# Transposes moved between VectorE and TensorE, and FFN pieces dealt by a table, in an RWKV-7 and hard-swish kernel

## The chip, the cores and the metric

The kernel runs on one core of a Trainium2 chip. The core has a matrix engine (TensorE, called PE in the profile; PEld is its weight load), a vector engine (VectorE, DVE), a scalar engine (ScalarE, ACT), GpSimd (POOL) and SyncE (SP), which only issues transfers. TensorE writes its results to PSUM; the other engines read them from there. Each engine runs its own instructions in the order of the program and waits for others by semaphores. The metric is the device time of one execution in microseconds (us).

## The reference

Six inputs r, k, v, w, a, b of shape (batch 4, heads 8, time 768, width 40) go through a recurrence over time. Its output is the input of a feed-forward layer (FFN) with hard-swish. All is float32.

```python
for t in range(S):
    kt, vt, rt = (k[:, :, t], v[:, :, t], r[:, :, t])
    wt, at, bt = (w[:, :, t], a[:, :, t], b[:, :, t])
    y[:, :, t] = np.einsum('bhd,bhde->bhe', rt, state)
    Sa = np.einsum('bhde,bhe->bhd', state, at)
    state_decay = state * wt[:, :, None, :] - np.einsum('bhd,bhe->bhde', Sa, bt)
    state = state_decay + np.einsum('bhd,bhe->bhde', vt, kt)
...
h = x @ w_in                                   # (3072, 320) @ (320, 2048)
g = h * np.clip(h + 3.0, 0.0, 6.0) / 6.0
return (g @ w_out).astype(np.float32)          # (3072, 2048) @ (2048, 320)
```

## The kernel before

Time is cut into 12 chunks of 64 steps and the batch into two pairs: 24 units, numbered 0 to 23, each one chunk of one pair with all 8 heads. `NU` = 4 units (two chunks of both pairs) form a group; `NK` = 24.

**A unit's work** has two halves, each a set of named stages. A stage is a generator: it issues TensorE's matmuls, yields, and then issues what empties PSUM.

`prepare(i)` needs no state and runs ahead. W turns w (time by width to width by time) and starts a cumulative product along time (a scan on VectorE); `gam` finishes the products `G` and their reciprocals `rg`. A, B and K turn a, b, k and multiply by these. F is the matrix a·b of a chunk, E is a·k with a mask, EV is E times v, `factor` makes the scaled k and b for the update of the state.

`step(i)` is the part with the state. RT and VT turn r and v; RT also scales the state. S turns the state; R is a times the state plus EV; U and UT apply the inverse of (1 + F) to R; C and H are masked products of r with v and with U; rS is r times the state; y adds up the output and the new state; `move` and `move2` carry the output into the FFN's layout `xt` by eight transfers, four from ScalarE's queue and four from SyncE's. `beside` copies v.

**Turns.** There are three ways to turn a matrix. `turn_pairs` (L524) is four whole 128x128 TensorE transposes into one PSUM bank. `turn_halves` (L534) is eight of half the rows, into a pair of banks shared through `ps_pair`. `turn_blocks` (L475, L478) is VectorE's own transpose in blocks of 32x32; it needs its input loaded in another layout by `fetch_blocks` (L464), which reads everything twice, with eight transfers for r and four for a instead of four and two. `blocked(name, i)` says from which unit on this way is used.

**The inverse** of a group of four units is made on VectorE by `invert`: a transpose `fb`, then 60 small products and sums (L801, L807), two transposes. It is a generator too and is advanced by `aside(n)`, n steps at a time. Two `third_block` parts follow on TensorE in the first two units of the next group.

**The FFN** is the generator `stream`. A job is half of the hidden width of one unit: `expand` (matmuls `h`, L1144; ScalarE's `gt`, L1159; VectorE's `gt`, L1160) and `contract` (matmuls `o`, L1185). It yields after some matmuls; what lies between two yields is called a piece. Eight pieces make a job. A unit's jobs can begin when its `move2` is issued. `pieces(n)` keeps a fraction and deals whole pieces.

**Order.** The first units are written out by hand. From unit 4 on, a loop goes over `i` and four blocks `j` per unit; m counts the blocks, 0 to 79. In a block, `a_block(m)` collects the stages due for the unit's own step (`OWN_STAGES`, six stages over six blocks, so that two units overlap) and for the units prepared ahead (`AHEAD_STAGES` or `CLOSE_STAGES`), in two parts: those that began at a block divisible by four, and the others. `together` first issues all matmuls of a part in the order `PRODUCTS`, then everything else in the order `RESULTS`. At most five PSUM banks are handed out before it empties what it has. Stages named in `TURNS` get a PSUM bank from a ring (`one` or half a pair); the others share pairs of banks. After the first part come half of the block's FFN pieces, then the second part, the third block if there is one, and the other half. The number of pieces follows from `rate`: 2.8, 3.5 or 4.5 a block, 6.2 while an inversion is under way, then with two or three inversion steps after each piece; the fraction is carried, and once `spread` is set (from unit 7) it counts 8/9.

Unit u from 8 on is prepared from block max(3(u - 8), 4(u - 9)) on.

Of the kernel before, what the change touches and what calls it, by code (L numbers as in the profile page):

```python
# [11 lines left out]
ALU = mybir.AluOpType  # L12
# [19 lines left out]
def kernel(  # L32
# [402 lines left out]

    def blocked(name, i):

        return i >= {"A": 2 * NU, "R": NU + 1}.get(name, NK)

    def fetch_blocks(name, x, b, g, fresh):  # L440

# [38 lines left out]
    def fetch(name, i, engine=None):  # L480

        if i is None or i >= NK:
            return
        x, crossed = {"W": (w, 0), "A": (a, 0), "B": (b, 0), "K": (k, 0), "R": (r, 1),
                      "V": (v, 1)}[name]
        if name == "V":
            t = values[i % AHEAD]
        else:
            t = placed.get((name, i))
            if (name, i) == ("R", 1):  # L490
                t = others["K"]
            t = t if t is not None else (others if i < 2 * NU and i % 2 and name != "R" else inputs)[name]
        g, p = names[i]
        if blocked(name, i):
            t = fetch_blocks(name, x, 2 * p, g, i == (NU + 1 if crossed else 2 * NU))
            data[i][name + "N"] = t
            return
        engines = engine or nc.sync
        for q in range(2):
            engine = engines[q] if isinstance(engines, tuple) else engines  # L500
            y = x[2 * p + q, :, g * BL:(g + 1) * BL, :]
            rows = slice(q * BL, (q + 1) * BL)
            if crossed:
                for s in range(2):
                    engine.dma_start(out=t[rows, 4 * s:4 * s + 4, 0:D],
                                     in_=y[s::2].rearrange("h t e -> t h e"))
            else:
                engine.dma_start(out=t[rows, :, 0:D], in_=y.rearrange("h t e -> t h e"))
        data[i][name + "N"] = t
# [69 lines left out]
    def prepare(i, F):  # L579
# [56 lines left out]

        def a_stage():
            at = o["at"] = grp.tile([P, NPR, P], F32, name="at", tag="at")
            if halves:
                nc.vector.memset(_ap(o["wm"][:], 0, [[HB + 1, 2 * NB + 1]]), 0.0)  # L640
                turn_blocks(at, o["AN"], "A")
                nc.gpsimd.tensor_tensor(out=at[:], in0=at[:], in1=o["G"][:], op=ALU.mult)  # L642
            else:
                x = turn_pairs(o["AN"])
                yield PE
                nc.vector.memset(_ap(o["wm"][:], 0, [[HB + 1, 2 * NB + 1]]), 0.0)
                nc.vector.tensor_tensor(out=at[:], in0=x[:], in1=o["G"][:], op=ALU.mult)
            fetch("A", following(i))

        def b_stage():  # L650
# [78 lines left out]
                fetch(name, following(i))  # L729

        def k_stage():
            x = turn_in(o["KN"], halves)
            yield PE
            kt = o["kt"] = turned("kt")
            for y, z, g in zip(parts_of(kt, halves), x, parts_of(o["rg"], halves)):
                nc.vector.tensor_tensor(out=y, in0=z, in1=g, op=ALU.mult)  # L736

        def e_stage():
# [141 lines left out]
    def step(i):  # L880
# [50 lines left out]

        def s_S():

            sp = ps_pair(4, SLOT) if halves else ps_any([P, 2, 2, P])
            for q in range(2):
                for j in range(2):
                    x = st[:, q, 2 * j:2 * j + 2, :].rearrange("p r d -> p (r d)")
                    if halves:
                        for s in range(2):
                            nc.tensor.transpose(out=sp[s][:, 2 * q + j, :], in_=x[half(s)],  # L940
                                                identity=ident[half(s), half(s)])
                    else:
                        nc.tensor.transpose(out=sp[:, q, j, :], in_=x, identity=ident[:])
            yield PE
            S = m["S"] = grp.tile([P, 2, 2, P], F32, name="S", tag="S", bufs=1)
            if halves:
                nc.scalar.activation(out=S[:].rearrange("p q j (s e) -> p s (q j) e", s=2), in_=sp[2], func=AF.Copy)  # L947
            else:
                nc.scalar.activation(out=S[:], in_=sp[:], func=AF.Copy)
# [141 lines left out]
        def s_move2():  # L1091
            for dst, src in m["moves"][4:]:
# [1 line left out]
            ready[i] = m["xt"]  # L1094
            yield from ()

        return {"RT": s_RT, "RT0": s_RT, "R": s_R, "VT": s_VT, "S": s_S, "U": s_U, "C": s_C, "UT": s_UT,
                "rS": s_rS,
                "sn": s_sn, "H": s_H, "y": s_y_sn if halves else s_y, "beside": s_beside, "move": s_move, "move2": s_move2}

# [294 lines left out]
    for _ in range(18):  # L1395
# [4 lines left out]

    OWN_STAGES = [["RT", "VT"], ["R", "C", "S", "beside"], ["U", "UT", "rS"], ["H"], ["y"],
                  ["move", "move2"]]
# [11 lines left out]
    FIRST_NARROW = PRODUCTS[len(TURNS)]  # L1416

    def together(stages):

        begun, banks = [], 0  # L1420

        def finish():
# [9 lines left out]
        for name in PRODUCTS:  # L1432
            if name == FIRST_NARROW and narrow and spread[0] and stages:
                narrow[0]()
            for stage in stages.get(name, []):
                if name in TURNS:
                    need = 2 * (open_half[0] is None) if ring[0][0] == "pair" else 1
                else:
                    width = WIDTH.get(name, NPR * BL)
                    need = 2 * (shared[0] is None or shared[1] + width > 512)  # L1440
                if banks + need > 5:
                    finish()
                    banks, need = 0, 1 if name in TURNS else 2
                banks += need
                rest = stage()
                next(rest)
                begun.append((name, rest))
        begun.extend((name, stage()) for name in stages if name not in PRODUCTS
                     for stage in stages[name])
        finish()  # L1450

# [3 lines left out]
    def a_block(m):  # L1455
# [4 lines left out]
            ahead[u, m] = prepared(u), CLOSE_STAGES if close else AHEAD_STAGES  # L1460
        if m % BLOCKS == 0 and m // BLOCKS + NU < NK:
            i = m // BLOCKS + NU
            first = [["RT" if blocked("R", i) else "RT0", "VT"]]
            own[i, m] = step(i), first + OWN_STAGES[1:]
# [24 lines left out]
    m = 0  # L1489
    for i in range(NU, NK):  # L1490
        spread[0] = i >= 2 * NU - 1
        for j in range(BLOCKS):
            rate, inversion = 3.5, 0
            if i + AHEAD >= NK + NU - 1:
                rate = 4.5
            if i < 2 * NU - 1:
                rate = 2.8
            parts = a_block(m)
            next(parts)
            if side or i % NU == NU - 1 and rate < 4:  # L1500
# [12 lines left out]
            m += 1  # L1513
    for _ in range(2):
        for _ in a_block(m):
# [35 lines left out]
```

## Time and profile before

| what | value |
|---|---|
| median of 3 runs | 803.71 us (803.26 to 806.04) |
| the profiled execution | 804.22 us, span 802.5 us |
| TensorE busy | 721.0 us, 90% of the span |
| VectorE busy | 510.0 us, 64% |
| ScalarE, GpSimd busy | 298.5 us (37%), 171.8 us (21%) |
| FFN matmuls `h` and `o` | 252.1 and 233.7 us of TensorE |
| inversion steps (L801, L807) | 66.5 and 66.5 us of VectorE |
| r's and a's VectorE transposes (L475, L478) | 14.3 and 11.1 us |
| mean granted TensorE clock | 0.953 |

The profile gives for each engine when it was busy, for each group of instructions its line, operation, operands, count, busy time and the mean of one, and for idle time the instruction that ended it. Busy time of a group of overlapping matmuls is the time that at least one of them ran, so it is less than count times mean. The granted clock is the share of full speed that TensorE was allowed.

### The profile page before, as it was taken

To read this page: it belongs to the slowest core of one execution; us is meant where nothing else is said; L and a number is where in the kernel's file an instruction comes from. 1 tells how busy PE (TensorE), PEld (TensorE's weight loads), DVE (VectorE), ACT (ScalarE), POOL (GpSimd) and SP (SyncE) were. 2 spreads that over 40 slices of the span, in tenths; PEclk is the share of its full clock that TensorE was granted. 3 is DMA by queue.
4 is the path that set the end of the run, shared out by engine and by line. 5 is a ranking of instruction groups with operands and counts; after the bars stand their busy time and mean duration, and the time that the engine had idled before them with its cause. 6 is when DMAs were issued, how large, how long until landed. Compare 5 with 4: busy or idle time off the path is not lost.

```text
span 802.5 us, 32704 instructions
## 1 busy us (share of the span) xinstructions
PE 721.0 (90%) x14416; PEld 604.6 (75%) x14416; DVE 510.0 (64%) x1024; ACT 298.5 (37%) x629; POOL 171.8 (21%) x316
## 2 busy tenths in 40 slices
PE   5735778999979989999999999999999999999998
PEld 4625666878757878787878778878778888888876
DVE  7898886688545599564799455899345983333110
ACT  2337661232533414443334442324443224322121
POOL 6403012321233321222212112213112202000000
PEclk9756978999989999999999999999999999999999
DMA  8673653420434331443323334323333112210000
GB/s 121 133 181 93 153 137 64 70 48 15 80 67 75 74 65 35 84 81 68 64 62 54 61 79 79 62 58 62 58 78 71 20 29 45 46 38 18 20 19 16
DMA packets 196733, 53.87 MB, mean 67 GB/s; under 512 B 179952, under 2 KB 195312, under 8 KB 196592
## 3 DMA queue, kind: packets, MB, share of 16 engines
q1 hardware_dynamic: 188968, 48.43, 31.0%
q10 hardware_dynamic: 7624, 3.36, 1.6%
q8 instruction: 113, 1.85, 1.0%
q14 instruction: 28, 0.23, 0.1%
HBM read 39.81 MB, written 3.93 MB: 55 GB/s over the span
## 4 chain that ended last, share of the span: by engine, by line
PE 55%; DVE 21%; issue 9%; DMA 5%; SPq 4%; ACT 3%; POOL 2%; ACTq 1%; POOLq 0%; DVEq 0%
PE h L1144 20%; PE o L1185 17%; PE pair L562 3%; DVE prod L801 3%; DVE x L807 3%; SPq L464 3%; PE pair L1040 3%; DVE prods L599 2%; DVE gt L1160 2%; DVE wm L610 2%; PE pair L958 1%; DMA W<-in_w_dram 1%; PE pair L534 1%; ACTq L1088 1%; PE pair L978 1%
## 5 line engine op out<-in xcount | busy, mean ns | idle before, releaser
L1144 PE MATMUL h<-xt,win 128*128 128x128 f32 (+1 forms) x2304 | 252.1, 284 | 8.0 <-DVE gt L1160 7.9
L1144 PEld LDWEIGHTS h<-xt,win 128*128 128x128 f32 (+1 forms) x2304 | 232.6, 193 | 26.5 <-issue 6.7
L1185 PE MATMUL o<-wout,gt 128*128 128x320 f32 x768 | 233.7, 448 | 0.0
L1185 PEld LDWEIGHTS o<-wout,gt 128*128 128x128 f32 x768 | 140.3, 193 | 52.0 <-issue 2.4
L1160 DVE SCALAR_TENSOR_TENSOR gt<-gt,h 128x512 f32<-128x512 f32 x96 | 62.1, 682 | 66.3 <-ACT gt L1159 66.0
L1159 ACT ACTIVATE gt<-h,three 128x512 f32<-128x512 f32 x96 | 62.4, 685 | 106.6 <-PE h L1144 82.0
L801 DVE TENSOR_TENSOR prod<-x 128x30 f32<-128x30 f32 (+9 forms) x180 | 66.5, 369 | 8.9 <-POOL x L786 3.4
L807 DVE TENSOR_TENSOR x<-x,prod 128x30 f32<-128x30 f32 (+9 forms) x180 | 66.5, 370 | 5.5
L1048 POOL TENSOR_TENSOR yg<-ys,gam 128x512 f32<-128x512 f32 x20 | 25.4, 1271 | 135.7 <-DVE ys L1047 95.6
L575 DVE COPY_PREDICATED store<-mask,pair 128x512 f32<-128x512 int32 x40 | 29.1, 727 | 31.8 <-PE pair L562 21.7
L722 POOL TENSOR_TENSOR KBt<-K,rgt 128x320 f32<-128x320 f32 x19 | 16.9, 887 | 146.8 <-ACT rgt L711 141.0
L599 DVE TENSOR_TENSOR_SCAN prods<-wm,start 128x528 f32<-128x528 f32 x24 | 33.6, 1406 | 17.7 <-ACT wm L596 17.3
L736 DVE TENSOR_TENSOR kt<-pair,rgam 128x512 f32<-128x512 f32 x19 | 13.1, 687 | 48.8 <-PE pair L702 48.4
L642 POOL TENSOR_TENSOR at<-at,gam 128x512 f32<-128x512 f32 x16 | 20.4, 1272 | 81.3 <-DVE at L478 77.4
L1047 DVE TENSOR_TENSOR ys<-pair,ys 128x512 f32<-128x512 f32 x20 | 13.8, 689 | 36.5 <-PE pair L1040 36.5
L755 ACT ACTIVATE EV<-pair 64x320 f32<-64x320 f32 x44 | 18.9, 431 | 40.1 <-PE pair L750 32.2
L1040 PE MATMUL pair<-store,KBt 64*64 64x104 f32 x1280 | 32.6, 250 | 0.5 <-DVE bt L655 0.5
L610 DVE TENSOR_TENSOR_SCAN wm<-wm,start 128x528 f32<-128x528 f32 x24 | 30.4, 1268 | 0.8
L1040 PEld LDWEIGHTS pair<-store,KBt 64*64 64x64 f32 x1280 | 29.2, 133 | 1.1 <-DVE bt L655 0.6
L1203 ACT ACTIVATE ob<-o 128x320 f32<-128x320 f32 x22 | 9.6, 436 | 53.9 <-PE o L1185 29.9
L869 ACT ACTIVATE tinv<-pair 32x256 f32<-32x256 f32 x48 | 18.0, 374 | 25.6 <-DMA xt<-yg 17.7
L947 ACT ACTIVATE S<-pair 128x512 f32<-128x512 f32 x20 | 11.9, 597 | 37.9 <-PE pair L534 22.2
(284 smaller groups left out, 1036.7 us busy)
## 6 DMA issues: line engine op xcount, KB each, us to landing
R<-in_r_dram SPq DMA_DIRECT2D x168, 40.0 KB
A<-in_a_dram SPq DMA_DIRECT2D x69, 80.0 KB
V<-in_v_dram SPq DMA_DIRECT2D x96, 40.0 KB
out_dram<-ob SPq DMA_DIRECT2D x47, 80.0 KB
B<-in_b_dram SPq DMA_DIRECT2D x42, 80.0 KB
store<-V SPq DMA_DIRECT2D x20, 160.0 KB
W<-in_w_dram SPq DMA_DIRECT2D x37, 80.0 KB
K<-in_k_dram SPq DMA_DIRECT2D x37, 80.0 KB
```

The costliest lines, as they stand in the source:

```text
L464: nc.sync.dma_start(out=t[rows, first + k * H * D:first + k * H * D + n * 2 * D].rearrange("p (n e) -> p n e", n=n), in_=y)
L575: nc.vector.copy_predicated(out=x[:, :, 0:BL].rearrange("p (h i) t -> p i h t", i=2), mask=mask8, data=o[2])
L599: nc.vector.tensor_tensor_scan(out=prods[:].rearrange("p r m i -> p (r m i)"), data0=wm[:, 0:SCAN], data1=start[:], initial=0.0, op0=ALU.m ...
L610: nc.vector.tensor_tensor_scan(out=back, data0=back, data1=start[:], initial=0.0, op0=ALU.mult, op1=ALU.add)
L801: nc.vector.tensor_tensor(out=pv, in0=_ap(x[:], (i + 1) * L + i, [[L, n], [0, i]]), in1=_ap(x[:], i * L, [[0, n], [1, i]]), op=ALU.mult,)
L807: nc.vector.tensor_tensor(out=rest, in0=rest, in1=pv, op=ALU.add)
L1040: nc.tensor.matmul(out=y[q][half(s), pr, :], lhsT=o[name][half(q), h * D:h * D + SLOT], rhs=m[name][half(q), x, :], start=(name == "K" and ...
L1048: nc.gpsimd.tensor_tensor(out=yg[:], in0=m["ys"][:].rearrange("p r q t -> p r (q t)"), in1=o["G"][:], op=ALU.mult)
L1144: nc.tensor.matmul(out=hp[c][:, i, :], lhsT=lhsT, rhs=rhs, start=(begun[c] == 0), stop=(begun[c] == 3 * NQ - 1))
L1159: nc.scalar.activation(out=gt[:], in_=hp[c][:], func=AF.Relu, bias=three[:], scale=1.0)
L1160: nc.vector.scalar_tensor_tensor(out=gt[:], in0=gt[:], scalar=6.0, in1=hp[c][:], op0=ALU.min, op1=ALU.mult)
L1185: nc.tensor.matmul(out=op[:], lhsT=gts[c][:, n, :], rhs=wout[:, c * HJ + r * NQ + n, :], start=((split or r == 0) and c == 0 and n == 0), ...
```

## The change

r is turned by VectorE from unit 8 on (before: 5), a from unit 12 on (before: 8). Between these, both are turned by TensorE in halves. k is turned in halves from unit 12 on (before: 8) and the state from unit 8 on (before: 4); until then both are turned whole, with a bank from the ring.

A stage of an earlier unit of such a kind gets another name (`RT1`, `A1`, `K1`, `S1`), and the order of the matmuls in a block is given by two lists, one for blocks 0 to 15, one for later blocks. The order of the results is changed too. `together` lists the ring's stages W, S1, K1 first.

The number of FFN pieces of each block is a digit of `GAPS`, and the number of inversion steps after each piece a digit of `INVERSION`; pieces are now taken from the stream directly, without the carried fraction. Half of a block's pieces come before the second part only where there is a third block or something in the second part; otherwise all come at the end.

```diff
     def blocked(name, i):
 
-        return i >= {"A": 2 * NU, "R": NU + 1}.get(name, NK)
+        return i >= {"A": 3 * NU, "R": 2 * NU}.get(name, NK)
...
         def a_stage():
             at = o["at"] = grp.tile([P, NPR, P], F32, name="at", tag="at")
-            if halves:
+            if blocked("A", i):
                 nc.vector.memset(_ap(o["wm"][:], 0, [[HB + 1, 2 * NB + 1]]), 0.0)
                 turn_blocks(at, o["AN"], "A")
                 nc.gpsimd.tensor_tensor(out=at[:], in0=at[:], in1=o["G"][:], op=ALU.mult)
             else:
-                x = turn_pairs(o["AN"])
+                x = turn_in(o["AN"], halves)
                 yield PE
                 nc.vector.memset(_ap(o["wm"][:], 0, [[HB + 1, 2 * NB + 1]]), 0.0)
-                nc.vector.tensor_tensor(out=at[:], in0=x[:], in1=o["G"][:], op=ALU.mult)
+                for y, z, g in zip(parts_of(at, halves), x, parts_of(o["G"], halves)):
+                    nc.vector.tensor_tensor(out=y, in0=z, in1=g, op=ALU.mult)
...
         def k_stage():
-            x = turn_in(o["KN"], halves)
+            by_halves = i >= 3 * NU
+            x = turn_in(o["KN"], by_halves)
...
         def s_S():
 
+            halves = i >= 2 * NU
...
-    PRODUCTS = ["W", "S", "B", "K", "factor", "VT", "RT0", "E",
-                "y", "R", "C", "U", "UT", "rS", "H", "EV", "F"]
-    RESULTS = ["RT", "RT0", "y", "W", "VT", "EV", "R", "S", "C", "A", "B", "move", "move2",
-               "U", "UT", "rS", "F", "K", "H", "E", "factor", "beside", "gam"]
-    TURNS = ["W"]
+    TURNS = ["W", "S1", "K1"]
+    NARROW = [["RT1", "VT", "A1", "B", "factor", "y", "EV", "R", "C", "U", "UT", "rS", "H", "E", "F", "K", "S"],
+             ["B", "A1", "S", "VT", "E", "U", "K", "C", "y", "factor", "H", "R", "UT", "RT1", "rS", "EV", "F"]]
+    RESULTS = ["C", "S", "RT1", "RT", "VT", "y", "S1", "R", "W", "A1", "move", "A", "EV", "B", "move2", "U",
+              "UT", "rS", "K", "H", "K1", "factor", "E", "gam", "F", "beside"]
+    FIRST_OTHER = {"RT": 2 * NU, "A": 3 * NU, "K": 3 * NU, "S": 2 * NU}
...
                 for name in order[m - begin]:
-                    parts[begin % BLOCKS > 0].setdefault(name, []).append(fs[name])
+                    kind = name + "1" if u < FIRST_OTHER.get(name, 0) else name
+                    parts[begin % BLOCKS > 0].setdefault(kind, []).append(fs[name])
         for k, part in enumerate(parts):
-            together(part)
+            together(part, m >= 16)
...
     def feed(n, inversion):
 
-        whole = int(n)
-        for k in range(whole):
-            pieces(1)
+        for _ in range(n):
+            next(stream)
             aside(inversion)
-        pieces(n - whole)
...
+    GAPS = "71052314311277562421243135343899422124213525759654324442543253966531154234264363"
+    INVERSION = "00000000000034230000000000221223000000000012232300000000001323230000000000122343"
     m = 0
     for i in range(NU, NK):
         spread[0] = i >= 2 * NU - 1
         for j in range(BLOCKS):
-            rate, inversion = 3.5, 0
-            if i + AHEAD >= NK + NU - 1:
-                rate = 4.5
-            if i < 2 * NU - 1:
-                rate = 2.8
+            amount, inversion = int(GAPS[m]), int(INVERSION[m])
             parts = a_block(m)
             next(parts)
-            if side or i % NU == NU - 1 and rate < 4:
-
-                rate, inversion = 6.2, 2 + (i < 2 * NU)
-            feed(rate / 2, inversion)
+            third_here = i % NU < 2 and j < 2
+            ahead_here = any(begin % BLOCKS and m - begin < len(order) and order[m - begin]
+                             for (u, begin), (_, order) in ahead.items())
+            first = amount // 2 if third_here or ahead_here else 0
+            feed(first, inversion)
             for _ in parts:
                 pass
-            if i % NU < 2 and j < 2:
+            if third_here:
                 if i % NU == 0:
                     aside(3 * L)
                 block(i, j)
-            if side:
-                rate, inversion = 6.2, 2 + (i < 2 * NU)
-            feed(rate / 2, inversion)
+            feed(amount - first, inversion)
             m += 1
```

More of the change, by code (lines that the diff above doesn't have):

```diff
@@ L494, in fetch @@
         if blocked(name, i):
[L495 removed]
+            t = fetch_blocks(name, x, 2 * p, g, i == (2 * NU if crossed else 3 * NU))
             data[i][name + "N"] = t
@@ L731, in k_stage @@
         def k_stage():
-            x = turn_in(o["KN"], halves)
+            by_halves = i >= 3 * NU
+            x = turn_in(o["KN"], by_halves)
             yield PE
             kt = o["kt"] = turned("kt")
-            for y, z, g in zip(parts_of(kt, halves), x, parts_of(o["rg"], halves)):
+            for y, z, g in zip(parts_of(kt, by_halves), x, parts_of(o["rg"], by_halves)):
                 nc.vector.tensor_tensor(out=y, in0=z, in1=g, op=ALU.mult)
@@ L1095, in s_move2 @@
             yield from ()
-        return {"RT": s_RT, "RT0": s_RT, "R": s_R, "VT": s_VT, "S": s_S, "U": s_U, "C": s_C, "UT": s_UT,
+        return {"RT": s_RT, "R": s_R, "VT": s_VT, "S": s_S, "U": s_U, "C": s_C, "UT": s_UT,
                 "rS": s_rS,
@@ L1398, with together @@
     aside(3 * L)
-    OWN_STAGES = [["RT", "VT"], ["R", "C", "S", "beside"], ["U", "UT", "rS"], ["H"], ["y"],
-                  ["move", "move2"]]
+    OWN_STAGES = [["RT", "VT"], ["R", "C", "S", "beside"], ["U", "UT", "rS"], ["H"], ["y"], ["move", "move2"]]
     AHEAD_STAGES = [["W", "gam"], ["A", "B"], ["F"], ["K", "factor"], ["E"], [], [], ["EV"]]
     CLOSE_STAGES = [["W", "gam"], ["A", "B"], ["F", "K", "factor"], ["E"], [], ["EV"]]
-    PRODUCTS = ["W", "S", "B", "K", "factor", "VT", "RT0", "E",
-                "y", "R", "C", "U", "UT", "rS", "H", "EV", "F"]
-    RESULTS = ["RT", "RT0", "y", "W", "VT", "EV", "R", "S", "C", "A", "B", "move", "move2",
-               "U", "UT", "rS", "F", "K", "H", "E", "factor", "beside", "gam"]
-    TURNS = ["W"]
+    TURNS = ["W", "S1", "K1"]
[4 more added lines that the diff above has]
+    FIRST_OTHER = {"RT": 2 * NU, "A": 3 * NU, "K": 3 * NU, "S": 2 * NU}
     WIDTH = {"R": NPR * D, "U": NPR * D, "y": NPR * BOTH, "EV": NPR * D}
     BLOCKS = 4
-    FIRST_NARROW = PRODUCTS[len(TURNS)]
-    def together(stages):
+    def together(stages, order):
         begun, banks = [], 0
+        products = TURNS + NARROW[order]
         def finish():
@@ L1430, in finish @@
             ring.extend(TURNS_IN)
-        for name in PRODUCTS:
-            if name == FIRST_NARROW and narrow and spread[0] and stages:
+        for name in products:
+            if name == NARROW[order][0] and narrow and spread[0] and stages:
                 narrow[0]()
@@ L1447, in together @@
                 begun.append((name, rest))
-        begun.extend((name, stage()) for name in stages if name not in PRODUCTS
+        begun.extend((name, stage()) for name in stages if name not in products
                      for stage in stages[name])
@@ L1462, in a_block @@
             i = m // BLOCKS + NU
-            first = [["RT" if blocked("R", i) else "RT0", "VT"]]
-            own[i, m] = step(i), first + OWN_STAGES[1:]
+            own[i, m] = step(i), OWN_STAGES
         parts = {}, {}
```

## The prediction

> **What bounds the kernel now.** I read the page's engine table and slices first, then the table by stretches of 20 us, then TensorE's waits, then the list in order of time around the longest idle places.
>
> From the page: busy shares, then the tenths of PE and the granted clock in 40 slices.
>
> ```profile
> PE 721.0 (90%) x14416; PEld 604.6 (75%) x14416; DVE 510.0 (64%) x1024; ACT 298.5 (37%) x629; POOL 171.8 (21%) x316
> ...
> PE   5735778999979989999999999999999999999998
> ...
> PEclk9756978999989999999999999999999999999999
> ```
>
> TensorE bounds it from about 200 us on. Its idle time is 53.5 us before 200 us, where the diff changes no instruction (the loop with the new tables begins at 197 us, with unit 4), and 25.5 us behind. So at most 25.5 us, and what a lowered clock costs, can be won by filling gaps. From the table by stretches (PE, PEld, DVE, ACT, POOL, then granted clock):
>
> ```profile
> 220.00:240.00 20.00, 14.90 (x382) 11.10 (x382) 8.92 (x18) 7.52 (x19) 6.60 (x10) 0.87 0.34 66
> 280.00:300.00 20.00, 17.71 (x253) 14.34 (x244) 18.83 (x45) 4.63 (x9) 6.03 (x13) 0.91 0.30 61
> 420.00:440.00 20.00, 20.00 (x332) 17.38 (x332) 18.26 (x37) 8.84 (x19) 5.78 (x7) 1.00 0.28 50
> ```
>
> 11.7 us of the idle time lie in 200 to 320 us, 12.5 us in 320 to 780 us, where most stretches are over 94% busy. Blocks can be told apart by the matmuls: block m=0 begins at 197.1 us (W of unit 8, r of unit 4), m=4 at 220.0, m=5 at 227.8, m=6 at 242.0, m=12 at 277.2, m=13 at 292.9. Blocks 5 and 12 take 14.3 and 15.6 us against 4 to 9 for the others. The list in order of time shows why:
>
> ```profile
> 231.56 0.60 ACT L947 ACTIVATE S<-pair 128x512 f32<-128x512 f32 x1
> ...
> 232.21 2.32 ACTq L1088 DMA_DIRECT2D xt<-yg  x3
> ...
> 234.57 0.37 ACT L689 ACTIVATE F<-pair 32x256 f32<-32x256 f32 x1 [2.41 <-DMA xt<-yg]
> ...
> 236.69 1.08 PE L859 MATMUL pair<-zs,tt 32*32 32x32 f32 x64 [3.15 <-ACT F L692]
> ...
> 237.70 4.42 PE L1185 MATMUL o<-wout,gt 128*128 128x320 f32 x8
> ```
>
> In block 5 ScalarE issues the four `move` transfers before it empties F; TensorE wants that PSUM pair and stands 3.15 us. The granted clock is then 0.50 from 235 to 241.6 us: the eight `o` instructions take 4.42 us, where eight take 2.42 at 221.99. In block 12 VectorE is behind:
>
> ```profile
> 282.04 0.77 DVE L475 STREAM_TRANSPOSE RT<-R 128x256 f32<-128x256 f32 x2
> ...
> 288.49 1.28 DVE L1160 SCALAR_TENSOR_TENSOR gt<-gt,h 128x512 f32<-128x512 f32 x2
> ...
> 289.24 3.83 PE L1144 MATMUL h<-xt,win 128*128 128x128 f32 x24 [2.29 <-DVE gt L1160]
> ```
>
> `gt` stands in VectorE's queue behind r's transposes, the state, a scan and `gam`; the next `h` waits for it 2.29 us, and the clock falls to 0.50 again.
>
> **The change, part by part.** The profiled execution took 804.22 us (span 802.5), 0.51 above the median of 803.71; the sum is made against it.
>
> *Transposes.* r of units 5, 6, 7 returns to TensorE: eight half turns each. The row L534 for V has 160 of them in 8.6 us, 0.43 us a unit, so 3 x 0.43 = +1.3. a of units 8 to 11: 4 x 0.43 = +1.7. k of units 8 to 11 goes from halves (7.0 us / 16 units = 0.44) to four whole turns (row L524 for W: 12.5 us / 19 units = 0.66): +0.9. The state of units 4 to 7 the same way (L940: 8.9 / 20 = 0.445): +0.9. TensorE's work grows by 4.8 us, all in blocks 0 to 13. At the top all of it is paid; at the bottom none, since that stretch has 11.7 us of idle. Blocks 0 to 7 hold about half of it and most of the idle; blocks 8 to 13 are nearly full, so I take half: **+2.4**.
>
> The Trainium skill, "TensorE: Matmul & The Clock Gate", Part 4 (PE-mode transpose), speaks against such a return: about 275 ns for one transpose in a kernel. The net count is 24 (r) + 32 (a) - 16 (k) - 16 (state) = 24 more instructions, so an estimate from that page is 6.6 us of work where the rows give 4.8, and the sum would be 0.9 higher. Row L534 has 54 ns for one when eight follow each other, so the trace does not agree for half turns.
>
> On the other engines: VectorE loses 0.75 us a unit (L475: 14.3 / 19) for r, and for a it swaps a 0.69 transpose (L478) for a 0.68 product read from PSUM (L647). ScalarE gains 0.6 a unit for r (L897), which lies in blocks 4, 8 and 12, where it has idle time. GpSimd loses 1.27 a unit for a (L642); it is 21% busy, so nothing. SyncE's queue: r's fetch goes from eight transfers to four, a's from four to two, 20 fewer of about 0.45 us; k, b, w, v and the second moves behind them leave 1 to 2 us earlier. r's fetch now waits for TensorE's turns in place of VectorE's; queued behind it are W and V for later units, which have a block or more in hand. Nothing taken for that. VectorE's 0.75 counts in block 12, where r's transposes stand ahead of the `gt` that TensorE waits for: between 0 and -0.75 plus the clock that follows (24 `h` took 3.83 us there, 2.94 at 274.43); I take **-0.75**.
>
> *Order in a block.* In block 5 the state's turn now has the single bank `one`, as has k's; EV, R share a pair and C has the next; `factor` and F share the first pair again, and the third block the second. ScalarE's order is S, the moves, EV, then `factor`, F. What TensorE waits for is thus EV, not F: S is emptied 1.4 us after the block begins, four issues take 3.07 (230.81 to 234.53 less S's 0.60), EV 0.86, so 5.3 us. TensorE has S 0.66, EV 0.57, R 0.49, C 0.60, one piece 1.27, k's turns 0.66: 4.25 us. It stands 1.1 us in place of 3.15 + 0.34, and so short an idle lowers the clock nowhere in blocks 6 to 11. So -2.4, and -2.2 of clock (2.0 at `o`, 0.2 at L859): **-4.6**, with 0 if the wait only moves. The state's turn at 258.7 us waits 1.08 us for F's pair; with a bank of its own **-1.0** (0 if R waits in its place). From block 16 on the two orders give nearly the same sequence; there only C goes before R, so RR is ready one copy (0.73) later, covered by the pieces behind block 1 of each unit (two to five of 1.27 us).
>
> *Pieces.* One FFN piece is (252.1 + 233.7) / 384 = 1.27 us. At block 0, 17 pieces of units 0 to 3 are left (counted from the `h` and `o` groups of blocks 0 to 5). The old rates deal 16 nominally by the end of block 5 (17 ran), the table 7, 1, 0, 5, 2, 3 = 18: both run dry there, and unit 4 gives the next work. Over all 80 blocks the rates give 306, the table 301; by sixteens 57, 64, 64, 64, 57 against 55, 63, 60, 65, 58. Five pieces (6.3 us) move to the tail, which is TensorE alone either way: no cost. Zero pieces in block 2 lay bare UT's way over ScalarE (1.05 us now): bounds 0 and +1.5, taken as 0.5, given back by seven pieces in block 0. Where a unit's first blocks have a third block, one or two pieces now stand ahead of it; it waited 2.0 us in all for the state after 320 us (rows of TensorE's waits, below). I take **-1.0** for these, between 0 and -5.
>
> ```profile
> PE pair L836 <- DVE state L1052: 2.0, 3, 0.9
> PE pair L682 <- issue: 2.8, 4, 1.1
> PE h L1144 <- DVE gt L1160: 2.6, 2, 1.3
> ```
>
> *Inversion steps.* Their number (67) stays. The rates spread them as 9, 18, 18, 18, 3 over blocks 11 to 15 and 12 a block later; the table has 21, 28, 10, 7 in blocks 12 to 15 and 49 of 67 in blocks 29 to 31. A step is 0.37 us (L801, L807), a piece's share of `gt` 2 x 0.68 / 8 = 0.17. At two steps a piece VectorE needs 0.91 us a piece, at three 1.28, at four 1.65, against TensorE's 1.27. In blocks 12 and 13 VectorE has some 29 us (46 steps 15.5, `fb` 2.2, the units' own 8.8, `gt` 2.6) against 23 on TensorE, and catches up in 14 and 15; today it is behind likewise (18.83 of 20 busy). I take **0**, between -3 (the 2.29 and its clock vanish) and +6 (all the lag shows).
>
> Sum: 804.2 + 2.4 - 0.75 - 4.6 - 1.0 - 1.0 + 0 = 799.3, less 0.5 for the median: **798.8**.
>
> **Rivals.** *It evens out:* the waits of block 5 and 258.7 us move to the next bank, and TensorE's idle there exists because unit 4's xt is not ready, whatever the order. Then 803.7 + 2.4 - 1 = 805, within 800.5 and 807.5. For it: FFN work has run dry there in both. Against: the clock was at 0.50 only where TensorE stood over 2 us.
>
> *Slower, by bunched inversion steps:* from three steps a piece on VectorE is the longer, `gt` falls behind, and `h` stands. Today one such stand costs 2.3 + 0.9 (3.83 against 2.94). If it comes in each of the four groups at twice that length and the clock falls each time, 4 x (4.6 + 0.9) - 3.2 = +19 at the worst, at half of that about +9; with +2.4 for the turns and, at the upper end, -4.6 for block 5: 808 to 820, likeliest near 812. Against: later groups have 26 pieces (33 us) and 7.6 us of attention matmuls over their last three blocks against 31 to 34 on VectorE.
>
> The same page of the Trainium skill, Part 1 (HAM oscillation), says that an idle of about 3.4 us halves the clock. By that rule block 5 keeps its clock if it stands 1.1 us; the trace agrees at 233 us (3.15 us idle, then 0.50), though 2.29 us was enough at 287.
>
> *More is filled:* half the 12.5 us idle after 320 us goes too: 798.8 - 6 = 793.
>
> **Chances.** Forecast 0.38 (own range 794 to 803), evens out 0.22, slower 0.30, more filled 0.10. A difference under 0.5% (4.0 us) is about what a measurement cannot tell from none: faster is below 799.7, slower above 807.7. The forecast gives faster 0.27 and same 0.11; evening out same 0.19, slower 0.03; bunching slower 0.27, same 0.03; more filled faster 0.10. So faster 0.37, same 0.33, slower 0.30. The range leaves out half of the lower case and a fifth of the slower: 791 to 813.
>
> **What would show it.** Right: TensorE's idle of 3.15 us around 234 us shrinks and the clock row stays at 1.00 there; L940's wait for F goes; TensorE's busy sum for the turns rises by 4 to 5 us; r's transfers fall from 168 to 156, a's SyncE issues by eight. Wrong: `h <- DVE gt` in TensorE's waits grows beyond 12 us in all (7.9 now), VectorE is full in 280 to 300 us and a clock under 0.9 shows there or at the later inversions; or TensorE's idle between 220 and 260 us stays at about 7 us.

## The result, and the profile after

| | before | after |
|---|---|---|
| median (of 4 runs each) | 803.93 us (803.26 to 806.04) | 793.06 us (792.22 to 796.25) |
| the profiled execution, its span | 804.22, 802.5 us | 793.15, 791.4 us |
| TensorE busy; mean granted clock | 721.0 us; 0.953 | 719.5 us; 0.954 |

The ratio after/before is 0.9868, with a 95% interval of 0.9835 to 0.9900: 1.3% faster, 10.9 us between the medians. The forecast was 798.8, about half of that gain. (The median of before is 803.71 over the three runs known at the prediction.)

The page of after, engine table and slices:

```profile
PE 719.5 (91%) x14440; PEld 608.4 (77%) x14440; DVE 507.2 (64%) x1018; ACT 298.1 (38%) x632; POOL 166.5 (21%) x312
...
PE   4725778999899898999999999999999999999998
...
PEclk9856879999999899999999999999999999999999
```

TensorE's work is nearly the same, so almost all of the gain is idle time. The table by stretches of after (PE, PEld, DVE, ACT, POOL busy, granted clock, DMA share, GB/s) shows that it did not simply vanish:

```profile
220.00:240.00 20.00, 18.61 (x527) 14.15 (x525) 8.48 (x16) 9.93 (x27) 5.67 (x9) 1.00 0.43 76
...
260.00:280.00 20.00, 19.08 (x337) 15.53 (x338) 12.26 (x24) 6.72 (x16) 8.02 (x16) 0.83 0.42 76
280.00:300.00 20.00, 18.78 (x329) 15.73 (x328) 18.22 (x44) 7.72 (x18) 2.86 (x7) 1.00 0.26 52
300.00:320.00 20.00, 16.22 (x225) 13.54 (x224) 16.93 (x38) 5.31 (x9) 4.21 (x6) 0.91 0.20 35
...
420.00:440.00 20.00, 19.91 (x359) 16.89 (x357) 16.94 (x31) 7.70 (x15) 6.53 (x10) 1.00 0.26 45
```

Most of the hole of 220 to 240 us has closed (14.90 busy before, clock 0.87). Two new low places stand behind it: the clock falls in 260 to 280 us, where it was 1.00, and 300 to 320 us has only 16.22 busy, where it had 19.57. Over 200 to 320 us the idle time is 11.7 us before and after, and the time at a clock of 0.50 is some 10 us in both (234.9 to 241.8 and 289.6 to 293.0 us before, 261.6 to 268.4 and 306.0 to 309.4 us after). The list in order of time of after, block 5 and then block 10:

```profile
229.24 0.60 ACT L952 ACTIVATE S<-one 128x512 f32<-128x512 f32 x1 [0.23 <-PE one L946]
229.32 3.74 ACTq L1091 DMA_DIRECT2D xt<-yg  x4
...
233.16 0.87 ACT L757 ACTIVATE EV<-pair 64x320 f32<-64x320 f32 x2 [3.33 <-DVE kt L738]
...
234.09 0.80 PE L861 MATMUL pair<-zs,tt 32*32 32x32 f32 x64 [0.66 <-ACT EV L757]
234.82 1.34 PE L1188 MATMUL o<-wout,gt 128*128 128x320 f32 x4
...
260.36 0.69 PE L997 MATMUL pair<-RT,S 40*64 40x64 f32 x32 [1.71 <-DVE score L571]
...
264.47 2.50 PE L1188 MATMUL o<-wout,gt 128*128 128x320 f32 x4
```

In block 5 ScalarE still issues its four transfers before it empties anything but S, but the third block (L861) now waits for EV, 0.66 us instead of 3.15 for F, and the next four `o` take their usual 1.34 us. In block 10 TensorE stands 1.71 us with one piece at hand, and the four `o` behind it take 2.50 us: the clock is low. In the first inversion, after:

```profile
304.52 0.35 DVE L809 TENSOR_TENSOR x<-x,prod 128x184 f32<-128x184 f32 x1
304.79 1.28 DVE L1163 SCALAR_TENSOR_TENSOR gt<-gt,h 128x512 f32<-128x512 f32 x2
305.53 3.71 PE L1147 MATMUL h<-xt,win 128*128 128x128 f32 x24 [3.78 <-DVE gt L1163]
```

The wait for `gt` behind VectorE's inversion steps has grown from 2.29 to 3.78 us, and the 24 `h` after it again take 3.7 where 2.94 is usual.

The late part filled up. One measure is used for that from here on, since at one moment the kernels have done different amounts of FFN: **net** is the change of the time at which a unit's y (the matmuls of 64x104) begins, less the change of the FFN work done by then (`h` 0.109 us each, `o` 0.302, from the groups' busy time). Negative is a gain. It comes from one profiled execution of each kernel, and those lie up to 3.1 us from their medians, so that single values say little under 3 us; differences within one execution are firmer. Between the y of unit 14 and that of unit 20 the stretch is, before and after:

```profile
517.09:687.77 170.68, 165.83 (x3337) 139.48 (x3329) 114.05 (x233) 63.99 (x135) 32.47 (x55) 1.00 0.26 52
```

```profile
499.85:673.74 173.89, 173.89 (x3422) 147.95 (x3412) 117.30 (x244) 64.63 (x138) 32.19 (x55) 1.00 0.27 53
```

4.85 us of idle became none, with more FFN in it; the net of this stretch is -8.3 us (from -1.6 to -9.9). So the after is no sum of small savings: it gains early, loses that again, and gains late. The experiments separate the three.

### The profile page after: what moved, and what is told of

Same layout as the page of the kernel before. It is cut to its first block, busy times and chain, and to the rows that moved or that the text cites. A ratio compares the mean times of both kernels' runs of the same rounds, so it can differ in the third digit from the quotient of the medians.

```text
span 791.4 us, 32710 instructions
## 1 busy us (share of the span) xinstructions
PE 719.5 (91%) x14440; PEld 608.4 (77%) x14440; DVE 507.2 (64%) x1018; ACT 298.1 (38%) x632; POOL 166.5 (21%) x312
## 4 chain that ended last, share of the span: by engine, by line
PE 71%; DVE 15%; issue 4%; DMA 3%; ACT 2%; SPq 2%; POOL 0%; ACTq 0%; DVEq 0%; POOLq 0%
PE h L1147 25%; PE o L1188 24%; PE pair L562 4%; PE pair L1043 3%; DVE prod L803 3%; DVE x L809 3%; PE pair L534 2%; SPq L508 2%; DMA raw<-in_moe_w_out_dram 2%; PE pair L961 2%; PE one L524 1%; DVE prods L599 1%; PE pair L997 1%; PE pair L981 1%; PE pair L921 1%
## 5 line engine op out<-in xcount | busy, mean ns | idle before, releaser
L1188 PE MATMUL o<-wout,gt 128*128 128x320 f32 x768 | 229.7, 443 | 0.8 <-ACT ys L1003 0.8
L599 DVE TENSOR_TENSOR_SCAN prods<-wm,start 128x528 f32<-128x528 f32 x24 | 34.1, 1428 | 12.4 <-ACT wm L596 12.0
L642 POOL TENSOR_TENSOR at<-at,gam 128x512 f32<-128x512 f32 x12 | 15.2, 1269 | 65.5 <-DVE at L478 61.5
L950 ACT ACTIVATE S<-pair 128x512 f32<-128x512 f32 x16 | 9.6, 597 | 48.1 <-DVE store L575 27.2
L932 ACT ACTIVATE VT<-pair 128x512 f32<-128x512 f32 x22 | 13.1, 598 | 33.4 <-PE pair L562 18.0
L783 DVE STREAM_TRANSPOSE fb<-F 128x1024 f32<-128x1024 f32 x6 | 13.0, 2159 | 17.8 <-ACT F L693 15.7
```

The lines of the kernel that those rows point to most:

```text
L599: nc.vector.tensor_tensor_scan(out=prods[:].rearrange("p r m i -> p (r m i)"), data0=wm[:, 0:SCAN], data1=start[:], initial=0.0, op0=ALU.m ...
L1188: nc.tensor.matmul(out=op[:], lhsT=gts[c][:, n, :], rhs=wout[:, c * HJ + r * NQ + n, :], start=((split or r == 0) and c == 0 and n == 0), ...
```

## The experiments

Three sets of parts can be put in or left out: the *turns* (who turns r, a, k and the state, with the ring's banks that belong to it), the *orders* (`NARROW`, `RESULTS`) and the *tables* (`GAPS`, `INVERSION`, the new splitting). The theory held at first was that of the prediction: the order in block 5 carries the gain, and the tables are worth little. The rivals: the tables carry it ("more is filled"); or the turns do, through VectorE or through the banks. Every ratio is to the kernel before on the same chip.

| kernel | median, us | ratio (95%) |
|---|---|---|
| e1: tables alone | 805.58 | 1.0007 (0.9988 to 1.0025) |
| e2: after without tables | 793.29 | 0.9859 (0.9836 to 0.9881) |
| e3: after without orders | 795.49 | 0.9887 (0.9859 to 0.9916) |
| e4: after without turns | 813.10 | 1.0110 (1.0074 to 1.0146) |
| e5: after, old rates up to block 15 | 796.17 | 0.9918 (0.9891 to 0.9945) |
| e6: turns alone | 795.01 | 0.9902 (0.9873 to 0.9932) |
| e7: r alone | 800.68 | 0.9974 (0.9957 to 0.9991) |
| e8: a alone | 802.78 | 0.9994 (0.9979 to 1.0009) |
| e9: k and state alone | 795.20 | 0.9886 (0.9861 to 0.9911) |
| e10: e5, two pieces fewer in block 15 | 791.44 | 0.9846 (0.9816 to 0.9877) |
| e11: k alone | 797.89 | 0.9922 (0.9893 to 0.9951) |
| e12: after, steps less bunched at the start | 795.02 | 0.9875 (0.9845 to 0.9905) |

**e1 to e4: one set of parts in or out.**

e1 is before with the tables:

```diff
-            feed(rate / 2, inversion)
+            first = amount // 2 if third_here or ahead_here else 0
+            feed(first, inversion)
...
-            feed(rate / 2, inversion)
+            feed(amount - first, inversion)
```

> The kernel before with only the two tables and the new splitting of a block's pieces; turns and orders as before. If the tables fill TensorE's idle time of the later units (theory: pieces), the time is 793 to 798 us and TensorE's idle time between 320 and 780 us falls from 12.5 to under 6 us. If the order in a block does it, the time stays at 801 to 806 us with 10 us or more idle there. If the turns of units 4 to 11 do it, 800 to 805 us, and the late idle time does not tell. The 3.15 us wait for F in block 5 should stay.

Measured: no difference (805.58). The waits show that block 5 is untouched, and the stretches that the clock falls in blocks 1 and 2, which have one piece and none:

```profile
PE pair L859 <- ACT F L692: 3.1, 1, 3.1
```

```profile
205.00:210.00 5.00, 3.66 (x134) 3.37 (x133) 1.59 (x4) 0.60 (x1) 0.00 (x0) 1.00 0.36 67
210.00:215.00 5.00, 4.53 (x136) 4.06 (x123) 1.41 (x3) 1.94 (x6) 1.33 (x2) 0.66 0.48 98
215.00:220.00 5.00, 4.46 (x136) 4.34 (x138) 0.70 (x2) 3.19 (x10) 1.68 (x2) 0.50 0.17 29
```

The same digits do not always do this. After and e12 have them too, with the new turns and orders, stand 1.31 us at the same place (1.34 in e1) and keep the clock at 1.00; their net at unit 4 is +0.4 and -0.4, where e1 has +5.7. The net of e1 is +10.4 at unit 8, +11.5 at unit 14, +3.3 at unit 20: the tables lose early and win 8.2 us back late.

e2 is after with the old rates and the old splitting:

```diff
-            amount, inversion = int(GAPS[m]), int(INVERSION[m])
+            rate, inversion = 3.5, 0
...
-            feed(first, inversion)
+            if side or i % NU == NU - 1 and rate < 4:
+                rate, inversion = 6.2, 2 + (i < 2 * NU)
+            feed(rate / 2, inversion)
```

> The changed kernel with the old rates in place of the tables; turns and orders are the new ones. Theory pieces: 799 to 804 us, late idle time of TensorE 9 to 13 us. Theory order: 792 to 797 us with under 6 us of late idle time. The wait in block 5 should be short (under 1.5 us) in either, since the order and the banks set it; the wait of h for gt at the first inversion should be 2 us or less, since the steps are not bunched.

Measured: as fast as after. The clock does not fall once behind 200 us, and the net is -9.9 at unit 8, where after has +0.1; but from unit 14 to 20 it moves by only -1.1, and idle remains there:

```profile
504.79:674.36 169.57, 165.98 (x3337) 139.69 (x3328) 113.80 (x233) 64.38 (x137) 32.52 (x55) 1.00 0.27 52
```

So the tables' small sum is two large terms: about ten microseconds lost up to unit 8 and seven to eight gained from unit 14 to 20. The clock is a large part of the first: after spends 10.2 us at 0.50 behind 200 us, which is 5.1 us of work, and the profiles of e6, e9 and e11, which have the old rates as well, also keep 1.00 from 200 to 780 us.

e3 is after with the old orders of matmuls and results:

```diff
-    NARROW = [["RT1", "VT", "A1", "B", "factor", "y", "EV", "R", "C", "U", "UT", "rS", "H", "E", "F", "K", "S"],
...
+    NARROW = 2 * [["S", "B", "A1", "K", "factor", "VT", "RT1", "E", "y", "R", "C", "U", "UT", "rS", "H", "EV", "F"]]
...
```

> The changed kernel with the old order of the products and of the results (new turns and tables stay). Theory order: 799 to 804 us, and the wait for F of about 3 us with a lowered clock returns in block 5, worth 4 to 5 us. Theory pieces: 793 to 797 us, at most the 4 us of block 5 lost.

Measured: 795.49; its interval overlaps that of after. Block 5's wait did not come back. So the orders did not remove it; what they add, 0.0019 of the ratio here (1.5 us) and 0.0043 between e6 and e2 (3.5 us), is within the intervals, which between e6 and e2 only just overlap.

e4 is after with the old limits for the turns:

```diff
-        return i >= {"A": 3 * NU, "R": 2 * NU}.get(name, NK)
+        return i >= {"A": 2 * NU, "R": NU + 1}.get(name, NK)
...
-            by_halves = i >= 3 * NU
+            by_halves = i >= 2 * NU
...
-            halves = i >= 2 * NU
+            halves = i >= NU
...
-    FIRST_OTHER = {"RT": 2 * NU, "A": 3 * NU, "K": 3 * NU, "S": 2 * NU}
+    FIRST_OTHER = {"RT": NU + 1}
```

> The changed kernel with the old limits: r by VectorE from unit 5, a from unit 8, k in halves from unit 8, the state in halves from unit 4; tables and orders are the new ones. If the added TensorE turns (4.8 us of work) cost what the rows say and half of it is paid, this is 1 to 4 us faster than the changed kernel: 789 to 792 us. If the turns relieve VectorE, SyncE or the banks of blocks 0 to 15, it is slower: 795 to 800 us.

Measured: slower than before, 813.10, but this is no clean test of the turns. In the first of the new lists k stands behind `factor` and F. With k no longer in the ring, five banks are handed out in block 2 before k's turn comes; what has begun is emptied first, and that includes the fetch of the next unit's k. Unit 8's k is then turned from the buffer that unit 9's has gone into: this kernel computes unit 8's E from unit 9's k, and TensorE waits for that transfer:

```profile
PE pair L534 <- DMA K<-in_k_dram: 5.3, 2, 5.0
PE pair L534 <- ACT EV L757: 2.9, 1, 2.9
```

What it shows is that the new order needs k's own bank. The turns had to be tested the other way.

**e6 to e9, e11: the turns alone, one by one.** All five have the old order (as in e3) and the old rates (as in e2). e6 has the new limits of all four; against before:

```diff
-        return i >= {"A": 2 * NU, "R": NU + 1}.get(name, NK)
+        return i >= {"A": 3 * NU, "R": 2 * NU}.get(name, NK)
...
+            by_halves = i >= 3 * NU
+            x = turn_in(o["KN"], by_halves)
...
+            halves = i >= 2 * NU
             sp = ps_pair(4, SLOT) if halves else ps_any([P, 2, 2, P])
...
+    TURNS = ["W", "S1", "K1"]
```

The others undo some of them. For e11, k alone, against e6:

```diff
-        return i >= {"A": 3 * NU, "R": 2 * NU}.get(name, NK)
+        return i >= {"A": 2 * NU, "R": NU + 1}.get(name, NK)
...
-            halves = i >= 2 * NU
+            halves = i >= NU
...
-    FIRST_OTHER = {"RT": 2 * NU, "A": 3 * NU, "K": 3 * NU, "S": 2 * NU}
+    FIRST_OTHER = {"RT": NU + 1, "K": 3 * NU}
```

e7 keeps only R's `2 * NU`, e8 only A's `3 * NU`, e9 K's and S's.

> The kernel before with only the new turns (old orders, old rates). If the turns alone carry the gain: 793 to 797 us. If they need the new orders: 799 to 804 us.

> The kernel before with only r of units 5 to 7 turned by TensorE. If VectorE's 0.75 us a unit and the twelve transfers of SyncE's queue matter most: 798 to 801 us. If the gain comes from a, k or the state: 802 to 805 us.

> The kernel before with only a of units 8 to 11 turned by TensorE in halves (GpSimd's product and eight transfers fall away). If a's way over VectorE and GpSimd to F held up the early blocks: 798 to 801 us, and the wait of the third block for F in block 5 shrinks. If not: 803 to 806 us, with 1.7 us more work for TensorE.

> The kernel before with only k of units 8 to 11 and the state of units 4 to 7 turned whole, in banks of the ring. Theory banks: the wait of the third block for F in block 5 (3.1 us, then the clock at 0.50) is gone, because k and the state no longer share pairs, and the time is 796 to 799 us, although TensorE's turns got 1.8 us longer. Rival: the gain of the turns is VectorE's and SyncE's relief through r and a together; then 803 to 806 us and the wait stays.

> The kernel before with only k of units 8 to 11 turned whole in a bank of the ring. Theory banks: k is what shares a pair with factor in block 5 and pushes F into the pair that the third block needs next, so k alone removes the 3.1 us wait and its lowered clock: 797 to 800 us. If the state's turn does it: 802 to 805 us and the wait stays.

Measured: the turns alone give 0.9902, most of the change. r alone gives 0.9974 and a alone nothing (0.9994); in both, block 5 keeps its wait of 3.1 or 3.2 us for F. k and the state alone give 0.9886, k alone 0.9922, and in both the wait is gone. The list of e11 in block 5 shows how:

```profile
230.70 0.60 PE L524 MATMUL one<-ident,K 128*128 128x128 f32 x4
...
231.70 0.69 PE L683 MATMUL pair<-bt,at 40*64 40x64 f32 x32
232.32 1.19 PE L861 MATMUL pair<-zs,tt 32*32 32x32 f32 x64
233.44 2.42 PE L1188 MATMUL o<-wout,gt 128*128 128x320 f32 x8
233.50 0.37 ACT L690 ACTIVATE F<-pair 32x256 f32<-32x256 f32 x1 [2.35 <-DMA xt<-yg]
```

F is emptied as late as ever, behind ScalarE's transfers (2.35 us). But k's turn now takes a bank of the ring (`one`) and no longer a share of a pair, so `factor` and F move into one pair and the third block gets another, which is free. It runs 1.2 us before F is emptied, and the eight `o` behind it take 2.42 us, not 4.42. (A stage of the ring is also issued first in its part; but what ends the wait is the free pair, since F is not emptied sooner.) Nothing got faster; the wait had been for a place in PSUM. e11's net is -1.0 at unit 4, -5.5 at unit 5, -7.1 at unit 10 and -7.3 at unit 20: most of it won around one block and kept to the end.

**e5 and e10: where the late gain of the tables comes from.** e5 is after with the old rates in blocks 0 to 15 and the tables from 16 on. It should have joined e2's good start to after's good end.

```diff
-            feed(first, inversion)
+            if m < 16:
+                feed_rate(rate / 2, early_steps)
+            else:
+                feed(first, inversion)
```

> The changed kernel with the old rates in blocks 0 to 15 and the tables from block 16 on. Theory: the tables cost about 10 us in blocks 0 to 15 (bunched inversion steps, blocks with no piece, lowered clock) and win about 6 us after them. Then this has the early blocks of the run with the old rates and the late ones of the changed kernel: 784 to 788 us. Rival: early and late only trade FFN work, and the time stays at 792 to 794 us.

Measured: 796.17, net -7.6 at unit 8 but only -1.0 from unit 14 to 20. With the same table the late gain was gone. e5 comes to block 16 two pieces further in the FFN (632 `h` and 192 `o` instructions issued) than after (624 and 188). e10 takes those two pieces out of block 15 and gives the steps that are left at its end; against e5:

```diff
-            if m < 16:
+            if m == 15:
+                feed_rate(rate / 2 - 2.25, 0)
+                aside(9)
+            elif m < 16:
                 feed_rate(rate / 2, early_steps)
```

> The changed kernel with the old rates in blocks 0 to 15, two pieces fewer in block 15, and the tables from block 16 on. At block 16 it has then issued exactly the FFN matmuls that the changed kernel has (the run with the rates first and the tables afterwards was two pieces ahead). Theory phase: the tables help only where a job's beginning falls into the block for which they were made; then the late gain of about 9 us returns on top of the early one, 783 to 787 us. Rival: the early gain is lost again for another reason; 791 to 796 us.

Measured: 791.44, the lowest median of all, and from unit 14 to 20 the net moves by -8.0. The stretch of e5 and that of e10:

```profile
500.61:679.75 179.14, 175.12 (x3409) 147.82 (x3401) 117.83 (x244) 64.64 (x139) 31.93 (x55) 0.99 0.26 51
```

```profile
496.96:671.06 174.10, 174.08 (x3422) 148.03 (x3412) 117.42 (x244) 64.63 (x138) 32.19 (x55) 1.00 0.28 53
```

4.02 us of idle against 0.02, from two pieces' difference in what the FFN has done at block 16. The table therefore fits one phase of the FFN's jobs against the blocks, and it is this fit that pays: e1, e3 and e12, which have after's table throughout, have -8.2, -8.2 and -8.3 in this stretch; e2 and e6, with the old rates, -1.1 and -1.6. Which meeting of a job's part with which block does it was not traced further. The 783 to 787 us expected for both gains together was missed: of the net of -8.9 at unit 6, -4.5 is left at unit 14, before the late gain begins. Against after, e10's interval overlaps, so it is not shown to be the better kernel; behind its nine steps in a row the third block waits 3.4 us, where after has its 3.78 for `gt`:

```profile
PE pair L838 <- DVE state L1055: 3.4, 1, 3.4
```

**e12: less bunching in the first inversion.** After with the steps of blocks 12 to 15 moved:

```diff
-    INVERSION = "00000000000034230000000000221223000000000012232300000000001323230000000000122343"
+    INVERSION = "00000000000023330000000000221223000000000012232300000000001323230000000000122343"
```

> The changed kernel with the inversion steps of blocks 12 to 15 spread as 14, 21, 15, 18 instead of 21, 28, 10, 18 (digits 2333 for 3423; nothing else). Theory bunching: the 3.8 us wait of h for gt near 302 us and the lowered clock behind it shrink, 789 to 792 us. Rival: the early loss of the tables comes from blocks with no or one piece alone; 792 to 795 us.

Measured: 795.02, no difference from after. The wait for `gt` of 3.78 us is gone, but the steps end later and the third block of the next unit waits for them:

```profile
PE pair L838 <- DVE state L1055: 5.2, 1, 5.2
```

```profile
315.00:320.00 5.00, 4.10 (x82) 3.84 (x84) 4.83 (x9) 1.50 (x4) 2.10 (x4) 0.56 0.51 98
```

VectorE is behind in these blocks either way, and the digits choose which of TensorE's matmuls wait for it. The early loss of the tables is therefore not mainly bunching. The largest part of it falls between unit 5 and 6, blocks 8 to 11, before any inversion step of the tables: net -5.8 to +0.2 in after, -7.8 to -8.7 in e2. There the tables deal 3, 1, 1 and 2 pieces where the rates deal 2.8 in each and some 4.5 in block 11, and block 10's stand and low clock, shown above, are in it. How much it costs varies by execution: e12 is the same program up to block 11, stands 1.32 us at that place where after stands 1.71, keeps its clock, and its net goes from -6.3 to -3.8. That few pieces are the cause is argued from the place; no run changed the pieces of these four blocks alone.

## Why the prediction was right, and where its sizes were off

- **The bound** was right: of the 11.1 us that the span lost, 1.5 are busy time of TensorE and 9.6 its idle time. Its size was a little off: TensorE's idle time behind 200 us was not 25.5 but 28.0 us (802.5 less 721.0, less 53.5).
- **Transposes, +2.4.** The work did grow: the turns' rows by 4.1 us in all (r 0.4 to 1.8, a 0 to 1.9, k's halves 7.0 to 5.2 and wholes 2.3 to 4.7, the state's halves 8.9 to 6.7 and wholes 2.4 more). But almost none of it was paid: a alone, 1.9 us of it, measures -0.5 (0.9994, less than can be told from none). The lower end, 0, was the better value. The 54 ns of a half turn is busy time over count; one record in that row lasts 226 ns, and they overlap.
- **VectorE, -0.75 in block 12.** The wait was right: in e7 the `h` of block 12 waits 1.54 us for `gt`, 0.75 less than the 2.29 before. r alone is worth 0.26% or 2.1 us after paying for its turns, but that is not shown to come from block 12. The net of e7 is already -2.3 at unit 5, where its low clock in block 5 lasted 3.4 us in place of 6.9, and moves by -0.9 from unit 6 to unit 8. Its granted clock is 1.00 in 280 to 300 us, where before had 0.91; so is that of e11, in which VectorE still turns r.
- **Order in a block, -4.6 and -1.0.** The size in block 5 was right: from unit 4 to unit 5 the net moves by -4.5 in e11 and by -6.2 in after. So was what is late next: 1.1 us forecast for EV, 0.66 measured. L940's wait of 1.08 us for F's pair went too. The name was half wrong: the step listed new banks and a new order together, and e3, e6 and e11 show that the banks do it and the order is not needed. The step also stopped at block 11. k and the state alone are worth 1.14%, or 9.2 us, 2.9 more than k alone; where those lie was not measured.
- **Pieces, -1.0.** This term failed, though its net was near the truth. The text put +0.5 on the one block without pieces and let seven pieces give it back, and put nothing on blocks 8 to 11. In after the first was near (net +0.4 at unit 4; in e1 the clock fell there, and it is +5.7). But from unit 5 to 6 after loses 6.0, with TensorE's stand and the low clock of block 10, and up to unit 8 the tables lose about ten against e2. The gain of at most 5 behind 320 us is one of seven to eight from unit 14 to 20, and not only at third blocks waiting for the state: those waits were 0.5 of the 4.85 us of idle in that stretch before.
- **Inversion steps, 0.** Right within its range as a sum (e12: moving them changes nothing that can be measured). The lag did show, as 3.78 us in one place, but `h <- DVE gt` fell from 7.9 to 5.8 us over the whole span. So the rival of bunched steps, with a stand in each of four groups, did not come: behind the first group no wait is long, as the largest two rows of TensorE's waits (after, 325 to 780 us) show:

```profile
PE pair L562 <- DVE start L608: 1.4, 2, 1.0
PE pair L838 <- DVE state L1055: 1.2, 2, 0.7
```

- **The rivals.** "It evens out" is refuted in block 5: the wait did not move to the next bank. "More is filled", 793 with a chance of 0.10, is the time that came, but not as it was added up: the late idle did fall, from 12.4 to 3.7 us over 320 to 780 us, and the tables lost as much early. e2 has the same time with 8.2 of that idle left.
- **Signs named.** The 3.15 us shrank to 0.66 with the clock at 1.00; r's transfers are 156 and a's 61 (eight fewer).

```profile
R<-in_r_dram SPq DMA_DIRECT2D x156, 40.0 KB
...
A<-in_a_dram SPq DMA_DIRECT2D x61, 80.0 KB
```

  The signs for being wrong did not show: the idle of about 7 us in 220 to 260 is 1.39 us in each of its halves, `h <- DVE gt` is 5.8 us, and the clock is 1.00 in 280 to 300 us.

The measured -10.9 against -4.9 is then: the turns with their banks about -8 (e6) where the terms of the turns, VectorE and order gave -4.0, and the rest between the orders and the tables, each of which is within the intervals. That the time lies so near to 793 is in part luck: two terms of the tables that the sum did not have, an early loss and a late gain, nearly cancel.

## What to carry to other kernels

Before costing a reordered queue, write down which PSUM bank each result gets and who empties the one before: a result that is emptied late costs nothing as long as nobody needs its bank, and giving one producer a bank of its own was worth more here than the new orders. A table that deals background work to stretches should be judged stretch by stretch, against work done and not against the clock alone, since two large terms can hide in a sum of zero. Such a table is tuned to one phase: changing anything ahead of it, even to the good, can void it (e5), so it is set last.

## What the runs showed of the hardware that was not expected

- The length of a stand does not decide alone whether the clock falls. Between 200 and 780 us of the fourteen profiled executions, every stand of TensorE of 1.99 us or more came with a granted clock of 0.50. Stands of 1.3 to 1.8 us came with it in some (1.71 us at 258.6 us in after, 1.66 at 203.8 in e8, 1.34 at 208.3 in e1) and not in others (1.79 us at 282.1 in e11, 1.78 at 281.5 in e9, and 1.32 at 258.2 in e12, at the same place of the same code as in after). The prediction had 2.29 us as the shortest that does; that a stand of 1.1 us would not lower it held in block 5 (0.66 us). The stretches of after:

```profile
258.00:260.00 2.00, 0.64 (x44) 0.50 (x36) 1.58 (x2) 1.31 (x4) 0.19 (x1) 1.00 0.55 103
260.00:262.00 2.00, 1.64 (x54) 1.58 (x56) 1.91 (x6) 0.60 (x1) 1.90 (x5) 0.90 0.12 28
262.00:264.00 2.00, 2.00 (x35) 1.78 (x36) 1.59 (x5) 0.49 (x1) 0.27 (x2) 0.50 0.67 116
```

  The Trainium skill, "TensorE: Matmul & The Clock Gate", Part 1 (A second HAM failure mode), tells of a kernel in which frequent short idles between groups of matmuls, while banks of PSUM are cycled, make the clock oscillate. The trace of after agrees with that in kind (1.71 us of idle, then 0.50), where the rule of about 3.4 us that the prediction cited does not cover it.
- The lowered clock outlasts its cause. In these executions each low spell between 200 and 780 us lasts 3.41 us or a whole multiple of it: 6.83 and 3.41 us in before and in after, 13.65, 3.41, 3.41 and 6.83 in e1, 3.41 in e7. So the stand of 1.71 us in after, with 6.83 us at half the clock, cost another 3.4 us of work; filling such a stand can be worth more than its length.
